# Letting the last batch's slots enter the slot product as one-hot products, in a kernel of clustered attention and a routed mixture of experts

## Chip, cores and metric

The kernel runs on one core of a Trainium2 chip. The metric is the device time of one execution in microseconds (us), as the median of several runs. About 0.2% of it, 1.5 us, can be told from no change.

## What is computed

The reference, cut to what matters here. `B, H, S, D = 4, 8, 768, 64`, so there are N = 3072 tokens of 512 values; 16 clusters; 4 groups of 4 experts, each with `w1` of 512 x 1024 and `w2` of 1024 x 512.

```python
# attention, for every batch and head
mask = q_assign[:, :, :, None] == k_assign[:, :, None, :]      # nearest centroids
scores = np.where(mask, scale * q @ k.T, -1e9)
x = softmax(scores) @ v                                        # -> tokens (N, 512)
# experts
for g in range(4):
    for e in range(4):
        ye = np.maximum(x[mine] @ w1[g, e], 0.0) @ w2[g, e]    # tokens whose group is g and expert e
        out[mine] = (g_w * e_w)[mine, None] * ye
```

## The kernel before

**Attention** (`attention`) goes through 32 heads of 9 units each; a unit is a piece of scores, its exponential (`exp` on ScalarE) and the product with V, and what is done beside the units (`beside`) is handed out unit by unit: a generator that yields once goes on one unit later. When the four head pairs of a batch are done, its 768 tokens are stored to `xbuf` in DRAM and routed.

**Routing** (`Router.decide`): for each batch the expert of each token is found, and its place among all tokens of its expert. The table in DRAM has for each expert a list of slots, and a slot holds a token's number and its gate. Each batch writes its entries by six scatters from GpSimd's queue (line 685, 128 tokens each, `table<-pay,rdi`). Empty slots hold the number N and the gate 0.

**Experts** (`Experts`). After three of the four batches, `first` picks the expert with most tokens so far. Beside the last batch's attention it loads and splits that expert's weights into high and low halves (`split_beside`), reads its list of 288 slots back (`tabA`), casts it to `idA` and `gA` (lines 849 and 850), gathers the tokens and turns them into `xTA`. When attention ends, **part A** (`part_a`) runs this expert on these slots: eight steps of `up` (line 963) and eight of `down` (line 985). Beside part A, the last batch is routed, `order` ranks the other experts by their number of tokens, and the stream of their weights starts (`stream`, line 767, six chunks of 512 KB ahead, which waits for `ei`, the ranked list). **Part B** then runs the first expert on its tokens of the last batch, which are picked by one-hot products (`slots_b`, `tokens_b`, lines 1107 to 1133) and never leave the chip. After it, `ranks` goes through the other experts, rank 0 to 14, with 288 slots down to 160; overflow is left to a loop at the end.

The lists of all ranks come from one place, the **slot product** (`slots`, line 1143): `tb`, the first 384 slots of each expert read back from the table (line 1113), times the permutation `perm` of the ranks, into one bank of PSUM. `columns` casts the result to `ri` and `rg` (lines 1053 and 1054), and the three gathers of rank 0 (line 925) start. `tb` is read behind all 24 scatters (`R.reads`).

The order on each engine is fixed when the program is built, by a scheduler that works with estimated times; `issue_after(ins)` adds that what is issued inside it on the engine of `ins` comes behind `ins`. `with self.after():` does this with the last `exp`. The wait lists, queues and buffers do the rest at run time: an engine's queue and SP's queue of transfers are in order, and `st` has four buffers, later six.

Of the kernel before, what the change touches and what calls it, by code (L numbers as in the profile page):

```python
# [22 lines left out]
P = 128  # L23
# [8 lines left out]
LAND = 4  # L32
# [496 lines left out]
class Router:  # L529
# [98 lines left out]
    def decide(self, b, early=None, then=None):  # L628
        nc, sm, E = self.nc, self.sm, self.E
        T = self.N // self.B // P  # L630
        t0 = b * T
        G = T * 5
        lv, eq, oh, df = (self.lg[b][:, n * G * 4:(n + 1) * G * 4].rearrange("p (g x) -> p g x", x=4) for n in range(4))
        mx = sm.tile([P, G], F32, name="rmx")
        nc.vector.tensor_reduce(out=mx, in_=lv, axis=AX.X, op=ALU.max)
        nc.vector.tensor_tensor(out=eq, in0=lv, in1=mx.broadcast_to([P, G, 4]), op=ALU.is_ge)
        nc.vector.tensor_tensor(out=eq, in0=eq, in1=self.desc[:, 0:G], op=ALU.mult)
        mw = sm.tile([P, G], F32, name="rmw")
        nc.vector.tensor_reduce(out=mw, in_=eq, axis=AX.X, op=ALU.max)
        nc.vector.tensor_tensor(out=oh, in0=eq, in1=mw.broadcast_to([P, G, 4]), op=ALU.is_equal)  # L640
        oh = oh.rearrange("p (t g) x -> p t g x", g=5)
        oe = sm.tile([P, T, 4, 4], F16, name="roe")
        og = sm.tile([P, T, 4], F32, name="rog")
        nc.vector.tensor_copy(out=og, in_=oh[:, :, 0])
        nc.vector.tensor_tensor(out=oe, in0=oh[:, :, 1:5], in1=og.broadcast_to([P, T, 4, 4]), op=ALU.mult)
        nc.vector.tensor_tensor(out=df, in0=lv, in1=mx.broadcast_to([P, G, 4]), op=ALU.subtract)
        nc.scalar.activation(out=df, in_=df, func=AF.Exp, scale=1.0 / (XS * WRS))
        se = sm.tile([P, T, 5], F32, name="rse")
        nc.vector.tensor_reduce(out=se.rearrange("p t g -> p (t g)"), in_=df, axis=AX.X, op=ALU.add)
        ss = sm.tile([P, T, 4], F32, name="rss")  # L650
        nc.vector.tensor_tensor(out=ss, in0=se[:, :, 1:5], in1=oh[:, :, 0], op=ALU.mult)
        yield
        es = sm.tile([P, T], F32, name="res")
        nc.vector.tensor_reduce(out=es, in_=ss, axis=AX.X, op=ALU.add)
        nc.vector.tensor_scalar(out=es, in0=es, scalar1=1e-9, scalar2=None, op0=ALU.add)
        nc.vector.scalar_tensor_tensor(out=es, in0=se[:, :, 0], scalar=1e-9, in1=es, op0=ALU.add, op1=ALU.mult)
        nc.vector.reciprocal(out=self.pay[:, t0:t0 + T, 1], in_=es)
        yield PSM, 1, 1
        o16 = oe.rearrange("p t g x -> p (t g x)")
        rk = self.psm.tile([P, 512], F32, name="psm")  # L660
        W = T * E
        nc.tensor.matmul(out=rk[:, 0:W], lhsT=self.low, rhs=o16, start=True, stop=False, skip_group_check=True)
        for s in range(1, T):
            nc.tensor.matmul(out=rk[:, s * E:W], lhsT=self.ones, rhs=o16[:, 0:W - s * E], start=False, stop=False, skip_group_check=True)
        for c in range(T):
            nc.tensor.matmul(out=rk[:, W:W + E], lhsT=self.ones, rhs=o16[:, c * E:(c + 1) * E], start=False, stop=c == T - 1, skip_group_check=True)
        yield
        ps = sm.tile([P, T, E], F32, name="rps")
        nc.vector.tensor_tensor(out=ps, in0=rk[:, 0:W].rearrange("p (t e) -> p t e", e=E), in1=self.cb.unsqueeze(1).broadcast_to([P, T, E]), op=ALU.add)
        nc.vector.tensor_tensor(out=ps, in0=ps, in1=oe.rearrange("p t g x -> p t (g x)"), op=ALU.mult)  # L670
        ds_ = self.rows = sm.tile([P, T], F32, name="rds")
        nc.vector.tensor_reduce(out=ds_, in_=ps, axis=AX.X, op=ALU.add)
        di = sm.tile([P, T], I32, name="rdi", bufs=2)
        self.last["v"] = nc.vector.tensor_copy(out=di, in_=ds_)
        nc.vector.tensor_tensor(out=self.cb, in0=rk[:, W:W + E], in1=self.cb, op=ALU.add)
        if early:
            early()
        if then:
            then()
        for c in range(T):  # L680
            for _ in range(1 if early else 4 if then else 5):
                yield

            with self.tc.issue_after(self.cfg["lo"].ins) if self.apart and not early and "lo" in self.cfg else ExitStack():
                d = self.last["p"] = nc.gpsimd.indirect_dma_start(
                    out=self.table, out_offset=bass.IndirectOffsetOnAxis(ap=di[:, c:c + 1], axis=0),
                    in_=self.pay[:, t0 + c], in_offset=None)
            if self.apart:

                self.alone(d, "sent", self.sent)  # L690
        self.done = b
# [17 lines left out]
class Experts:  # L709
# [4 lines left out]

    CA, CB = 288, 128
    AHEAD = 6
    SLOTS = 13
    SLT = 12
    FILL, SETTLE, TOK = (0, 1, 2, 3, 4, 5, 6, 7), 2, 5
# [20 lines left out]
    def setup(self):  # L740
        nc, const, E = self.nc, self.const, self.R.E
        self.io = const.tile([P, E], F32, name="io")
        nc.gpsimd.iota(self.io, [[1, E]], base=0, channel_multiplier=0, allow_small_or_imprecise_dtypes=True)
        self.capr = const.tile([1, E], F32, name="capr")
        i = 0
        while i < E:
            j = i
            while j < E and self.caps[j] == self.caps[i]:
                j += 1
            nc.gpsimd.memset(self.capr[:, i:j], float(self.caps[i]))  # L750
            i = j


    def part(self, i, q):
# [50 lines left out]
    def first(self):  # L805
# [15 lines left out]
        yield  # L821
        self.f0 = self.load_reg(self.f0i[0:1, 0:1], E - 1)
        self.WA = self.wtiles(self.wa, 0)
        chunks = []
        for q in range(4 + LAND):
            if q < 4:
                chunks.append(self.load_chunk(0, self.f0, q))
            if q >= LAND:
                yield from self.split_beside(chunks[q - LAND], *self.WA, 0, q - LAND)
            for _ in range(FIRST):  # L830
                yield

        CA, KD = self.CA, R.KD
        nt = -(-CA // P)
        sz = [min(P, CA - t * P) for t in range(nt)]
        tab = self.small("tabA", [P, nt, 2])
        tv = R.table.rearrange("(e s) w -> e s w", s=R.BS)[bass.ds(self.f0, 1)].rearrange("e s w -> (e s) w")
        w2A = [self.load_chunk(1, self.f0, q) for q in range(4)]
        self.WA += self.wtiles(self.wa, 1)
        while R.done < R.B - 2:  # L840
            yield
        for t, n in enumerate(sz):
            R.reads(nc.sync.dma_start(out=tab[0:n, t], in_=tv[t * P:t * P + n]))
        for _ in range(FIRST + 8):
            yield
        ids = self.small("idA", [P, nt], I32)
        g = self.small("gA", [P, nt])
        for t, n in enumerate(sz):
            nc.vector.tensor_copy(out=ids[0:n, t:t + 1], in_=tab[0:n, t, 0:1])
            nc.vector.tensor_scalar(out=g[0:n, t:t + 1], in0=tab[0:n, t, 1:2], scalar1=1.0 / (XS * WS * WS), scalar2=None, op0=ALU.mult)  # L850
        self.colsA = [g[0:n, t:t + 1] for t, n in enumerate(sz)], [ids[0:n, t:t + 1] for t, n in enumerate(sz)]

        rows = R.N - R.N // R.B
# [1 line left out]
        for t, n in enumerate(sz):  # L855
# [3 lines left out]
            if rows:  # L859
                with self.tc.issue_after(self.cfg["lo"].ins) if "lo" in self.cfg else ExitStack():  # L860
                    self.gather(ids[0:n, t:t + 1], n, xgs[t], rows)
            yield from self.split_beside(w2A[t], *self.WA[2:4], 1, t)
        for q in range(nt, 4):
            yield from self.split_beside(w2A[q], *self.WA[2:4], 1, q)
        xTA = self.wa.tile([P, KD, 2, CA], F16, name="xTA")
# [194 lines left out]
    def order(self):  # L1060
# [9 lines left out]
        nc.vector.scalar_tensor_tensor(out=key, in0=self.oh0, scalar=-1e7, in1=key, op0=ALU.mult, op1=ALU.add)  # L1070
        gt = sm("gt", [P, E, E], F16)
        nc.vector.tensor_tensor(out=gt, in0=key.unsqueeze(1).broadcast_to([P, E, E]), in1=key.broadcast_to([P, E, E]), op=ALU.is_gt)
        rank = sm("rank", [P, E])
        nc.vector.tensor_reduce(out=rank, in_=gt, axis=AX.X, op=ALU.add)
        pr = self.pr = sm("pr", [1, E, E])
        iob = self.io[0:1].broadcast_to([1, E, E])
# [17 lines left out]
    def slots_b(self):  # L1094
# [13 lines left out]
        nc.scalar.copy(out=self.o16, in_=o32)  # L1108
        self.o32, self.pb = o32, pb
        next(self.fill)  # L1110
        nt = self.nt = -(-max(self.caps) // P)
        self.tb = self.stage2.tile([P, 2, 512], F32, name="tb", bufs=1).rearrange("p a b -> p (a b)")[0:E, 0:2 * nt * P].rearrange("e (s w) -> e s w", w=2)
        R.reads(nc.sync.dma_start(out=self.tb, in_=R.table.rearrange("(e s) w -> e s w", s=R.BS)[0:E, 0:nt * P]))

    def tokens_b(self):

# [19 lines left out]
    def slots(self):  # L1136
# [3 lines left out]
        tpv = tps[:, 0:2 * nt * E].rearrange("p (w t e) -> p w t e", w=2, t=nt)  # L1140
        for t_ in range(nt):
            for w in range(2):
                nc.tensor.matmul(out=tpv[:, w, t_], lhsT=tb[:, t_ * P:(t_ + 1) * P, w], rhs=perm, start=True, stop=True)
        self.ids, self.gates = self.columns([tpv[:, 0], tpv[:, 1]], [P, nt, E], "r")
        self.xg0 = self.gathers(0)

# [229 lines left out]
def tile_cluster_attention_moe(ctx, tc, qT, kT, vr, cen, wr, w1, w2, out):  # L1376
# [33 lines left out]
    for _ in R.decide(B - 1, early=X.order):  # L1410
        pass
    X.slots_b()
    for i, _ in enumerate(ga):
        with tc.issue_after(X.mm.ins):
            if i == X.SLOTS:
                X.slots()
            if i == X.SLT:
                X.xTB = X.tokens_b()
# [38 lines left out]
```

## Time and profile before

| | |
|---|---|
| median of 3 runs | 769.58 us (769.55 to 770.92) |
| profiled execution, its own time | 770.8 us |
| its span, first to last instruction | 768.7 us |
| PE busy, matmuls (PE) and weight loads (PEld) | 94% and 81% |
| VectorE (DVE), ScalarE (ACT), GpSimd (POOL) busy | 78%, 58%, 64% |
| mean granted clock of PE | 0.981 |
| moved by DMA | 134.75 MB, 175 GB/s on average |

The trace counts from the first instruction of the span. Attention fills it to some 417 us, part A to some 457, part B to some 467 and the ranks the rest. A busy share is a mean over these stages, which have different limits, so the rows below are of single stretches.

### The profile page before, as it was taken

What the parts mean: (1) busy time and instruction counts of PE and PEld (TensorE: products, weight loads), DVE (VectorE), ACT (ScalarE), POOL (GpSimd) and SP (SyncE); (2) the same over time, 40 slices, a digit from 0 to 9 for tenths busy, and PEclk for the clock granted to TensorE, in tenths of its full rate; (3) what the DMA queues carried; (4) which work ended last, traced back from release to release, by engine and by line L of the source; (5) the groups of instructions that cost most, each with busy time, mean ns of one, the idle gap of its engine ahead of it and who ended that gap; (6) DMA issues with size and microseconds to landing.
All of it is one profiled execution on the core that took longest, in us unless ns stands there. A gap on an engine that the chain in (4) does not pass through costs nothing. (4 is left out here: it accounts for less than half of the span.)

```text
span 768.7 us, 26315 instructions
## 1 busy us (share of the span) xinstructions
PE 724.7 (94%) x10882; PEld 619.0 (81%) x10882; DVE 598.9 (78%) x1194; ACT 444.6 (58%) x877; POOL 495.7 (64%) x522
## 2 busy tenths in 40 slices
PE   5898999999999999997898979999999999999996
PEld 3676888888888888876776857888779999999896
DVE  5997988899798988996665545868588988888761
ACT  4567867677686777755674246444534455555542
POOL 9568687889978998787852435426555555554433
PEclk9999999999999999999989979999999999999998
DMA  8759647467653765407422487866677788788721
GB/s 248 190 157 217 161 125 158 111 145 185 125 162 91 173 146 104 97 12 178 127 63 61 55 269 275 275 210 216 226 245 239 255 255 274 256 279 276 248 75 49
DMA packets 115719, 134.75 MB, mean 175 GB/s; under 512 B 34963, under 2 KB 85651, under 8 KB 115592
## 3 DMA queue, kind: packets, MB, share of 16 engines
q1 hardware_dynamic: 109820, 119.61, 56.7%
q0 software_dynamic: 5616, 13.35, 4.9%
q8 instruction: 87, 1.43, 0.8%
q14 instruction: 40, 0.33, 0.2%
q10 hardware_dynamic: 156, 0.03, 0.0%
HBM read 93.20 MB, written 14.11 MB: 140 GB/s over the span
## 5 line engine op out<-in xcount | busy, mean ns | idle before, releaser
L354 POOL TENSOR_TENSOR pl<-p 128x512 f16<-128x512 f32 x278 | 285.6, 1047 | 80.8 <-ACT p L352 75.8
L308 DVE TENSOR_REDUCE mpart<-psc 128x1 f32<-128x512 f32 (+1 forms) x282 | 190.0, 683 | 29.2 <-PE psc L305 28.5
L352 ACT ACTIVATE p<-psf 128x512 f32<-128x512 f32 x288 | 168.5, 593 | 76.5 <-PE psf L348 69.4
L373 PE MATMUL pso<-V,p 128*128 128x65 f16 x1152 | 164.0, 195 | 0.0
L373 PE MATMUL pso<-V,pl 128*128 128x65 f16 x1152 | 163.2, 195 | 0.0
L374 PE MATMUL pso<-V,p 128*128 128x64 f16 x1152 | 162.9, 192 | 0.0
L374 PE MATMUL pso<-V,pl 128*128 128x64 f16 x1152 | 162.6, 192 | 0.0
L347 PE MATMUL psf<-A 82*128 82x384 f16 (+2 forms) x576 | 145.9, 278 | 6.4 <-ACT p L352 3.8
L348 PE MATMUL psf<-B 128*128 128x384 f16 (+2 forms) x576 | 146.1, 278 | 0.0
L374 PEld LDWEIGHTS <-p 128*128 128x128 bf16 x1152 | 113.6, 99 | 21.1 <-issue 1.0
L373 PEld LDWEIGHTS <-p 128*128 128x128 bf16 x1152 | 113.2, 98 | 12.6 <-issue 4.6
L305 PE MATMUL psc<-A 80*128 80x512 f16 (+1 forms) x376 | 109.9, 334 | 5.3 <-DVE mpart L308 4.2
L374 PEld LDWEIGHTS <-pl 128*128 128x128 f16 x1152 | 113.7, 99 | 0.6 <-issue 0.2
L373 PEld LDWEIGHTS <-pl 128*128 128x128 f16 x1152 | 112.1, 97 | 0.3
L966 DVE SCALAR_TENSOR_TENSOR hl<-psh,hh 128x160 f16<-128x160 f32 (+14 forms) x136 | 50.2, 371 | 60.5 <-ACT hh L965 60.1
L965 ACT ACTIVATE hh<-psh 128x160 f16<-128x160 f32 (+14 forms) x136 | 46.5, 347 | 62.5 <-PE psh L963 62.2
L963 PE MATMUL psh<-xT,wh0a 128*128 128x288 f16 (+7 forms) x512 | 74.7, 255 | 0.0
L348 PEld LDWEIGHTS <-B 128*128 128x128 f16 x576 | 57.4, 100 | 15.8 <-issue 6.6
L925 POOL DMA_INDIRECT xg<-xbuf,ri x32 | 42.2, 1318 | 40.9 <-issue 19.8
L963 PE MATMUL psh<-xT,wh0b 128*128 128x272 f16 (+6 forms) x448 | 65.2, 254 | 1.3 <-DVE xT L937 0.7
L347 PEld LDWEIGHTS <-A 82*128 82x128 f16 x576 | 56.2, 99 | 11.5 <-DMA A<-mr 2.2
L963 PE MATMUL psh<-xT,wl0a 128*128 128x288 f16 (+7 forms) x256 | 64.0, 255 | 0.0
(303 smaller groups left out, 1688.4 us busy)
## 6 DMA issues: line engine op xcount, KB each, us to landing
st<-w SPq DMA_DIRECT2D x128, 512.0 KB
B<-parts SPq DMA_DIRECT2D x64, 192.0 KB
kx<-kT SPq DMA_DIRECT2D x16, 384.0 KB
qx<-qT SPq DMA_DIRECT2D x16, 384.0 KB
vx<-vr SPq DMA_DIRECT2D x16, 384.0 KB
A<-parts SPq DMA_DIRECT2D x32, 192.0 KB
xbuf<-xs SPq DMA_DIRECT2D x16, 384.0 KB
A<-mk SPq DMA_DIRECT2D x56, 24.0 KB
```

Of the source, the lines that this page charges most:

```text
L305: last["mm"] = nc.tensor.matmul(out=pc[:, off:off + k1 - k0], lhsT=QA[h % 8][0:80, c * P:(c + 1) * P], rhs=KA[h % 8][0:80, k0:k1], start=T ...
L308: nc.vector.tensor_reduce(out=(mp[:, 0, 0:1], mp[:, :, 1], mp[:, 1, 0:1])[i], in_=pc.rearrange("p (a x) -> p a x", a=n), axis=AX.X, op=ALU ...
L347: nc.tensor.matmul(out=o, lhsT=KA[h % 8][0:82, ks], rhs=QA[h % 8][0:82, q0:q1], start=True, stop=False)
L348: nc.tensor.matmul(out=o, lhsT=KBs[h][:, ks], rhs=QBs[h][:, q0:q1], start=False, stop=True)
L352: cfg["exp"] = nc.scalar.activation(out=p32, in_=pf, func=AF.Exp, scale=QK / (SQ * SQ))
L354: lo = (nc.vector if u in (EARLY if h < 2 else DVE_LO[h % 8] if h < NH - 2 else DVE_END) else nc.gpsimd).tensor_tensor(out=pl, in0=p32, in ...
L373: nc.tensor.matmul(out=O[:, col:col + 65], lhsT=p[:, bs], rhs=vh, start=c == 0 and q == 0 and i == 0, stop=False, skip_group_check=True)
L374: nc.tensor.matmul(out=O[:, col:col + 64], lhsT=p[:, bs], rhs=vl, start=False, stop=c == NCH - 1 and i == 1, skip_group_check=True)
L925: self.got = nc.gpsimd.indirect_dma_start(out=xg[0:n].rearrange("p k a x -> p (k a x)"), out_offset=None, in_offset=bass.IndirectOffsetOnA ...
L963: self.mm = nc.tensor.matmul(out=ph[:, 0:M], lhsT=w[:, k, fs], rhs=xT[:, a, k], start=i == 0, stop=i == 3 * KD - 1)
L965: nc.scalar.activation(out=hh[:, f], in_=ph[:, 0:M], func=AF.Relu)
L966: self.ev = nc.vector.scalar_tensor_tensor(out=hl[:, f], in0=ph[:, 0:M], scalar=0.0, in1=hh[:, f], op0=ALU.max, op1=ALU.subtract)
```

## The change

The table is read into `tb` beside attention, when three batches are in it, and the fourth batch's entries are added to the slot product on TensorE:

- `slots_new` makes, on VectorE, for each of the last batch's six chunks of 128 tokens a one-hot of the slot within its expert (`oS`, 128 x 288) and a one-hot of its expert's rank times the token's number minus N and its gate. The number is cut into two and the gate into three bfloat16 parts (`sw`, three pairs). The pieces are handed out from step 5 of part A on.
- `slots` adds 54 matmuls (6 chunks x 3 slot tiles x 3 pairs) onto the product of `tb` and `perm`, in the same bank.
- The read of `tb` moves from `slots_b` into `first`, behind the gathers of part A's tokens, and its buffer out of the pool `stage2`.
- In `first`, the loads of the second weight matrix stand one by one behind the splits of the first one, no longer in one row behind all of them. The read of `tabA` comes one unit later, the casts after four units instead of ten and under `self.after()`.
- The last batch's six scatters stay, for the overflow loop.

```diff
@@ class Experts
+    ADD = 5
@@ setup
+        T = self.R.N // self.R.B // P
+        self.io16 = const.tile([P, max(self.caps)], F16, name="io16")
+        nc.gpsimd.iota(self.io16, [[1, max(self.caps)]], base=0, ...)
+        self.svals = const.tile([P, T, 3, 2], BF16, name="svals")
+        nc.gpsimd.memset(self.svals, 0.0)
+        nc.gpsimd.iota(self.svals[:, :, 0, 0], [[P, T]], base=-P * T, ...)
+        nc.gpsimd.iota(self.svals[:, :, 1, 0], [[0, T]], base=0, channel_multiplier=1, ...)
@@ first
             for _ in range(FIRST):
                 yield
+            if q >= LAND:
+                w2A.append(self.load_chunk(1, self.f0, q - LAND))
...
-        w2A = [self.load_chunk(1, self.f0, q) for q in range(4)]
         self.WA += self.wtiles(self.wa, 1)
         while R.done < R.B - 2:
             yield
+        yield
         for t, n in enumerate(sz):
             R.reads(nc.sync.dma_start(out=tab[0:n, t], in_=tv[t * P:t * P + n]))
-        for _ in range(FIRST + 8):
+        for _ in range(LAND):
             yield
...
-        for t, n in enumerate(sz):
-            nc.vector.tensor_copy(out=ids[0:n, t:t + 1], in_=tab[0:n, t, 0:1])
-            nc.vector.tensor_scalar(out=g[0:n, t:t + 1], in0=tab[0:n, t, 1:2], ...)
+        with self.after():
+            for t, n in enumerate(sz):
+                nc.vector.tensor_copy(out=ids[0:n, t:t + 1], in_=tab[0:n, t, 0:1])
+                nc.vector.tensor_scalar(out=g[0:n, t:t + 1], in0=tab[0:n, t, 1:2], ...)
...
+        self.nt = -(-max(self.caps) // P)
+        self.tb = self.small("tb", [R.E, self.nt * P, 2])
+        R.reads(nc.sync.dma_start(out=self.tb, in_=R.table...[0:R.E, 0:self.nt * P]))
@@ slots_b
-        nt = self.nt = -(-max(self.caps) // P)
-        self.tb = self.stage2.tile([P, 2, 512], F32, name="tb", bufs=1)...
-        R.reads(nc.sync.dma_start(out=self.tb, in_=R.table...[0:E, 0:nt * P]))
+    def slots_new(self):
+        nc, R, E, vals = self.nc, self.R, self.R.E, self.svals
+        T = R.rows.shape[1]
+        g = R.pay[:, R.N // P - T:, 1]
+        oe = R.oe.rearrange("p t g x -> p t (g x)")
+        x = self.small("sx", [P, T, E])
+        s = self.small("sslot", [P, T])
+        nc.vector.tensor_tensor(out=x, in0=oe, in1=R.ebase...., op=ALU.mult)
+        nc.vector.tensor_reduce(out=s, in_=x, axis=AX.X, op=ALU.add)
+        nc.vector.tensor_tensor(out=s, in0=R.rows, in1=s, op=ALU.subtract)
+        yield
+        self.oS = self.xp.tile([P, T, max(self.caps)], F16, name="hh")
+        for c in range(T):
+            nc.vector.tensor_scalar(out=self.oS[:, c], in0=self.io16, scalar1=s[:, c:c + 1], scalar2=None, op0=ALU.is_equal)
+            if c % 3 == 2:
+                yield
+        r = self.small("sg", [P, T])
+        nc.vector.tensor_copy(out=vals[:, :, 0, 1], in_=g)
+        nc.vector.tensor_tensor(out=r, in0=g, in1=vals[:, :, 0, 1], op=ALU.subtract)
+        nc.vector.tensor_copy(out=vals[:, :, 1, 1], in_=r)
+        nc.vector.tensor_tensor(out=r, in0=r, in1=vals[:, :, 1, 1], op=ALU.subtract)
+        nc.vector.tensor_copy(out=vals[:, :, 2, 1], in_=r)
+        yield
+        nc.vector.tensor_tensor(out=x, in0=oe, in1=self.rank...., op=ALU.mult)
+        rho = self.small("srank", [P, T])
+        nc.vector.tensor_reduce(out=rho, in_=x, axis=AX.X, op=ALU.add)
+        nc.vector.tensor_tensor(out=x, in0=self.io...., in1=rho...., op=ALU.is_equal)
+        yield
+        self.sw = self.small("sw", [P, T, 6, E], BF16)
+        nc.vector.tensor_tensor(out=self.sw, in0=x...., in1=vals...., op=ALU.mult)
@@ slots
-                nc.tensor.matmul(out=tpv[:, w, t_], lhsT=tb[:, t_ * P:(t_ + 1) * P, w], rhs=perm, start=True, stop=True)
+                nc.tensor.matmul(out=tpv[:, w, t_], lhsT=tb[...], rhs=perm, start=t_ + w == 0, stop=False, ...)
+        for t_ in range(nt):
+            for c in range(T):
+                for i in range(3):
+                    lhsT = self.oS[:, c, t_ * P:min((t_ + 1) * P, self.oS.shape[2])]
+                    nc.tensor.matmul(out=tpv[0:lhsT.shape[1], :, t_], lhsT=lhsT, rhs=self.sw[:, c, 2 * i:2 * i + 2], start=False, stop=c == T - 1 and i == 2, ...)
@@ main program
     X.slots_b()
+    new = X.slots_new()
     for i, _ in enumerate(ga):
         with tc.issue_after(X.mm.ins):
+            if i >= X.ADD:
+                next(new, None)
             if i == X.SLOTS:
```

## Rows read from the trace of the kernel before

**Rows 1.** The page's first line.
```profile
span 768.7 us, 26315 instructions
```

**Rows 2.** Windows over seven stretches; the header names the columns, PEclk is the granted clock.
```profile
core 0: us, PE busy (x) PEld busy (x) DVE busy (x) ACT busy (x) POOL busy (x), PEclk, DMA share, GB/s
385.00:391.90 6.90, 6.52 (x83) 5.19 (x83) 3.87 (x8) 2.64 (x6) 3.08 (x3) 0.51 0.01 2
408.90:412.30 3.40, 3.40 (x28) 2.46 (x27) 1.25 (x2) 2.43 (x5) 2.08 (x2) 0.50 0.00 0
434.00:440.00 6.00, 6.00 (x69) 5.14 (x67) 0.92 (x2) 0.82 (x2) 3.57 (x5) 1.00 0.99 152
443.90:449.10 5.20, 0.00 (x0) 0.00 (x0) 1.88 (x4) 2.79 (x4) 0.00 (x0) 0.75 0.87 226
449.10:456.70 7.60, 7.55 (x33) 5.76 (x34) 2.95 (x5) 0.00 (x0) 3.10 (x3) 0.50 0.78 247
486.00:680.00 194.00, 193.94 (x1998) 174.78 (x1996) 157.25 (x237) 91.88 (x183) 99.57 (x88) 1.00 0.77 248
680.00:724.00 44.00, 42.09 (x569) 41.24 (x567) 36.32 (x56) 21.30 (x49) 24.43 (x23) 1.00 0.80 266
```

**Rows 3.** Timeline of PE: start us, us, instruction, count, idle before and its releaser.
```profile
360.02 0.61 PE L609 MATMUL psm<-WR,xTr 128*128 128x20 f16 x18 [2.61 <-DMA xTr<-xs]
...
383.64 0.38 PE L305 MATMUL psc<-A 80*128 80x512 f16 x1 [2.45 <-DVE mpart L308]
...
407.50 0.41 PE L963 MATMUL psh<-xTA,wh 128*128 128x288 f16 x2 [2.38 <-DMA xTA<-vx]
...
412.97 0.60 PE L609 MATMUL psm<-WR,xTr 128*128 128x20 f16 x18
...
449.15 2.71 PE L1143 MATMUL psm<-perm,tb 16*128 16x16 f32 x12 [5.27 <-DMA tb<-table]
...
457.13 0.28 PE L963 MATMUL psh<-xT,wh 128*128 128x128 f16 x2
...
462.21 1.35 PE L935 MATMUL psm<-ident,xg 128*128 128x128 f16 x24
...
466.93 0.29 PE L963 MATMUL psh<-xT,wh0a 128*128 128x288 f16 x1
```

**Rows 4.** The chain of waits, 434 to 449 us: start us, us, what.
```profile
434.80 11.10 DMA table<-pay,rdi
...
446.01 3.01 DMA tb<-table
```

**Rows 5.** Timeline of VectorE (DVE), columns as in rows 3.
```profile
382.77 0.15 DVE L849 CAST idA<-tabA 128x1 int32<-128x1 f32 x1 [4.10 <-DMA tabA<-table]
...
428.50 0.27 DVE L1107 TENSOR_SCALAR st<-sl,rds 128x128 f32<-128x128 f32 x1
...
444.97 0.68 DVE L1126 CAST xT<-psm 128x512 f16<-128x512 f32 x1
...
451.90 0.21 DVE L1053 CAST ri<-psm 128x48 int32<-128x48 f32 x1 [6.12 <-PE psm L1143]
...
452.50 2.35 DVE L777 SCALAR_TENSOR_TENSOR wl0a<-st,wh0a 128x1024 f16<-128x1024 f32 x2
```

**Rows 6.** Line 609, 405 to 460 us: durations in ns, minimum, median, maximum.
```profile
L609 PEld LDWEIGHTS <-xTr x36: 95/96/99, 412.9 to 421.6; 128*128 128x128 f16 x36
L609 PE MATMUL psm<-WR,xTr x36: 171/171/185, 413.0 to 421.7; 128*128 128x20 f16 x36
```

**Rows 7.** Timeline of POOL, columns as in rows 3.
```profile
393.97 1.34 POOL L925 DMA_INDIRECT qx<-xbuf,idA  x1 [0.15 <-issue]
...
456.15 0.88 POOL L925 DMA_INDIRECT xg<-xbuf,ri  x1 [0.30 <-issue]
```

**Rows 8.** Line 925, the gathers of 440 to 480 us.
```profile
DMA to landing us min/median/max: 4.9/5.9/6.7
```

**Rows 9.** Timeline of SP's queue, columns as in rows 3.
```profile
356.14 8.51 SPq L767 DMA_DIRECT2D st<-w  x2
```

More of the change, by code (lines that the diff above doesn't have):

```diff
@@ L641, in decide @@
         oh = oh.rearrange("p (t g) x -> p t g x", g=5)
-        oe = sm.tile([P, T, 4, 4], F16, name="roe")
+        oe = self.oe = sm.tile([P, T, 4, 4], F16, name="roe")
         og = sm.tile([P, T, 4], F32, name="rog")
@@ L751, in setup @@
             i = j
+        T = self.R.N // self.R.B // P
+        self.io16 = const.tile([P, max(self.caps)], F16, name="io16")
+        nc.gpsimd.iota(self.io16, [[1, max(self.caps)]], base=0, channel_multiplier=0, allow_small_or_imprecise_dtypes=True)
+        self.svals = const.tile([P, T, 3, 2], BF16, name="svals")
+        nc.gpsimd.memset(self.svals, 0.0)
+        nc.gpsimd.iota(self.svals[:, :, 0, 0], [[P, T]], base=-P * T, channel_multiplier=0, allow_small_or_imprecise_dtypes=True)
+        nc.gpsimd.iota(self.svals[:, :, 1, 0], [[0, T]], base=0, channel_multiplier=1, allow_small_or_imprecise_dtypes=True)
     def part(self, i, q):
@@ L823, in first @@
         self.WA = self.wtiles(self.wa, 0)
-        chunks = []
+        chunks, w2A = [], []
         for q in range(4 + LAND):
@@ L847, in first @@
         g = self.small("gA", [P, nt])
-        for t, n in enumerate(sz):
-            nc.vector.tensor_copy(out=ids[0:n, t:t + 1], in_=tab[0:n, t, 0:1])
-            nc.vector.tensor_scalar(out=g[0:n, t:t + 1], in0=tab[0:n, t, 1:2], scalar1=1.0 / (XS * WS * WS), scalar2=None, op0=ALU.mult)
+        with self.after():
+            for t, n in enumerate(sz):
+                nc.vector.tensor_copy(out=ids[0:n, t:t + 1], in_=tab[0:n, t, 0:1])
+                nc.vector.tensor_scalar(out=g[0:n, t:t + 1], in0=tab[0:n, t, 1:2], scalar1=1.0 / (XS * WS * WS), scalar2=None, op0=ALU.mult)
         self.colsA = [g[0:n, t:t + 1] for t, n in enumerate(sz)], [ids[0:n, t:t + 1] for t, n in enumerate(sz)]
@@ L862, in first @@
             yield from self.split_beside(w2A[t], *self.WA[2:4], 1, t)
+        self.nt = -(-max(self.caps) // P)
+        self.tb = self.small("tb", [R.E, self.nt * P, 2])
+        R.reads(nc.sync.dma_start(out=self.tb, in_=R.table.rearrange("(e s) w -> e s w", s=R.BS)[0:R.E, 0:self.nt * P]))
         for q in range(nt, 4):
@@ L1072, in order @@
         nc.vector.tensor_tensor(out=gt, in0=key.unsqueeze(1).broadcast_to([P, E, E]), in1=key.broadcast_to([P, E, E]), op=ALU.is_gt)
-        rank = sm("rank", [P, E])
+        rank = self.rank = sm("rank", [P, E])
         nc.vector.tensor_reduce(out=rank, in_=gt, axis=AX.X, op=ALU.add)
@@ L1110, in slots_b @@
         next(self.fill)
-        nt = self.nt = -(-max(self.caps) // P)
-        self.tb = self.stage2.tile([P, 2, 512], F32, name="tb", bufs=1).rearrange("p a b -> p (a b)")[0:E, 0:2 * nt * P].rearrange("e (s w) -> e s w", w=2)
-        R.reads(nc.sync.dma_start(out=self.tb, in_=R.table.rearrange("(e s) w -> e s w", s=R.BS)[0:E, 0:nt * P]))
+    def slots_new(self):
[5 more added lines that the diff above has]
+        s = self.small("sslot", [P, T])
+        nc.vector.tensor_tensor(out=x, in0=oe, in1=R.ebase.unsqueeze(1).broadcast_to([P, T, E]), op=ALU.mult)
+        nc.vector.tensor_reduce(out=s, in_=x, axis=AX.X, op=ALU.add)
[13 more added lines that the diff above has]
+        yield
+        nc.vector.tensor_tensor(out=x, in0=oe, in1=self.rank.unsqueeze(1).broadcast_to([P, T, E]), op=ALU.mult)
+        rho = self.small("srank", [P, T])
+        nc.vector.tensor_reduce(out=rho, in_=x, axis=AX.X, op=ALU.add)
+        nc.vector.tensor_tensor(out=x, in0=self.io.unsqueeze(1).broadcast_to([P, T, E]), in1=rho.broadcast_to([P, T, E]), op=ALU.is_equal)
+        yield
+        self.sw = self.small("sw", [P, T, 6, E], BF16)
+        nc.vector.tensor_tensor(out=self.sw, in0=x.unsqueeze(2).broadcast_to([P, T, 6, E]), in1=vals.rearrange("p t i w -> p t (i w)").broadcast_to([P, T, 6, E]), op=ALU.mult)
     def tokens_b(self):
@@ L1142, in slots @@
             for w in range(2):
-                nc.tensor.matmul(out=tpv[:, w, t_], lhsT=tb[:, t_ * P:(t_ + 1) * P, w], rhs=perm, start=True, stop=True)
+                nc.tensor.matmul(out=tpv[:, w, t_], lhsT=tb[:, t_ * P:(t_ + 1) * P, w], rhs=perm, start=t_ + w == 0, stop=False, skip_group_check=True)
+        T = R.rows.shape[1]
+        for t_ in range(nt):
+            for c in range(T):
+                for i in range(3):
+                    lhsT = self.oS[:, c, t_ * P:min((t_ + 1) * P, self.oS.shape[2])]
+                    nc.tensor.matmul(out=tpv[0:lhsT.shape[1], :, t_], lhsT=lhsT, rhs=self.sw[:, c, 2 * i:2 * i + 2], start=False, stop=c == T - 1 and i == 2, skip_group_check=True)
         self.ids, self.gates = self.columns([tpv[:, 0], tpv[:, 1]], [P, nt, E], "r")
```

## Prediction

> **What bounds the kernel now.** Of the 768.7 us of the profiled execution [rows 1] PE is busy nearly all, and the page alone would say "PE bound, nothing to gain". So I read the windows first. They show that PE runs without a pause and at the full clock from 486 to 680 us [rows 2], so whatever makes PE start that stretch earlier moves everything behind it. [...] The timeline of PE names the place: line 1143, the slot product, starts at 449.15 after 5.27 us of idle, so PE had come there at 443.88 [rows 3]. The chain of waits names the reason: the transfer `table<-pay,rdi`, 11.10 us from its issue at 434.80, and behind it `tb<-table`, 3.01 us [rows 4]. So the six scatters of the last batch and the reading back of the table are what PE waits for in the middle of part A.
>
> Two smaller holes lie in the attention part. PE stands 2.45 us at 383.64, waiting for a VectorE reduction, and 2.38 us at 407.50, waiting for the transposed tokens `xTA` [rows 3]. After each the clock is at 0.50 to 0.51 for 6.9 and 3.4 us [rows 2]. The first has its cause on VectorE: the cast `idA` stood 4.10 us at the head of its queue until `tabA` landed, with the reductions behind it [rows 5].
>
> **The removed wait.** After the change, the table is read while only 18 scatters are behind it, long before 443.88. What does PE wait for then? Lines 1125 and 1129 and the slot product take their banks in turn from a pool of three, after `rk` of decide. Counting on from `rk`, the slot product takes the bank of the first product of line 1125, and VectorE empties that one at 444.97 + 0.68 = 445.65 [rows 5]. The 5.27 us shrink to 445.65 - 443.88 = 1.77 us, not to nothing.
>
> **The added matmuls.** Six chunks by three slot tiles by three parts are 54, with 128 x 128 weights and 32 columns. The nearest row is line 609: 18 matmuls with 20 columns in 0.60 us, of which the last one's 0.17 us is latency, so 0.43 / 17 = 25 ns each [rows 3, 6]. With 32 columns I take 28 ns: 1.5 us. The bound above is that no weight load overlaps anything: 54 x 96 ns = 5.2 us [rows 6]. I stay at 1.5, since line 609 issues a load of 96 ns for every matmul and still goes at 25 ns.
>
> [...]
>
> **PE up to the end of part A.** The twelve passes of line 1143 took 2.71 us at half clock [rows 3]; at full clock 1.36. From 449.15 + 2.64 = 451.79 to 457.13 the last 24 matmuls of line 985 took 5.34 us, of which all but the last 0.4 lay at half clock: 2.9 at full clock. An idle of 1.77 us is below the 2.38 to 5.2 us behind which the clock fell here, so I count full clock. New end: 445.65 + 1.36 + 1.5 + 2.9 = 451.4, against 457.13: 5.7 us earlier.
>
> **What is late next: the gathers of rank 0.** Its slot list leaves the slot product, VectorE casts it (line 1053, 451.90), and POOL issues three gathers, the third at 456.15, 4.25 us after the cast began [rows 5, 7]. The cast now begins at 445.65 + 1.36 + 1.5 + 0.05 = 448.6, the third gather at 452.8, and it lands 5.9 us later (4.9 to 6.7) [rows 8]: 458.7. PE needs it for the last eight transposes of line 935, which start 5.08 us after the end of part A [rows 3], some 0.4 of it in waits, plus 0.9 us for the two tiles before: 451.4 + 4.6 + 0.9 = 456.9 to 457.4. A new wait of about 1.3 us (0.3 to 2.1) appears. Left: 5.7 - 1.3 = 4.4 us.
>
> **Does it last to the end?** The first weights of rank 0 are split by 452.50 + 2.35 = 454.85 [rows 5], and before the change PE comes to them at 466.93 [rows 3], 12 us later, so they are ready. The weight stream itself moves too: its sixth load stood on SP's queue behind `tb`, issued at 446.01 [rows 4]; now only its buffer holds it, which is `o32`, read last by line 1129, ahead of PE's hole at 443.88. From 486 to 680 PE is full and DMA is at 0.77 [rows 2], so there is room; from 680 to 724 PE has 1.9 us of gaps, where the stream is just in time. I count 4.4 us as kept; if the stream did not follow, it would go there.
>
> **VectorE's new work.** Eighteen operations. Twelve at the 0.27 us of a 128-wide row and six over 288 columns at most 0.27 x 288 / 128 = 0.6: 3.2 + 3.6, at most some 7 us [rows 5]. Between 434 and 440 VectorE is busy for 0.92 of 6 us [rows 2], and PE needs the results at 445. Cost nothing; if they were put ahead of `ei`, which starts the weight stream, the stream would be late by some of it, inside the 12 us above. The four POOL operations in setup, by the same rule at most 0.6 each and 2.4 together, once and near the start, and the issue of `tb` on SP I count at nothing, since POOL and SP are not what PE waits for in any of the holes; bound 2.4 us.
>
> **The list of part A.** Two edits. The casts now stand under `after()`, which ties instructions to the last `exp`. `exp` is issued by `nc.scalar` and the casts run on VectorE [rows 5], and issue_after orders within one engine, so I expect no tie and the wait of 4.10 us to stay: 0. If it did bind, it would give up to 2.45 + 6.9 / 2 = 5.9 us. Second, ten units of waiting become four (and one before the read), so gathers and weight splits start some five units earlier than 393.97 [rows 7], and `xTA` is ready up to 8 us before PE stands at 407.50. This can remove 2.38 + 3.4 / 2 = 4.1 us. But the matmuls that wait there have a fixed place in PE's queue, which is made anew with the program and may lie as much earlier, with the same wait: 0. The trace can't tell; I take half, 2.0.
>
> **Sum.** 4.4 + 2.0 = 6.4 us. The profiled execution took 770.8 us (span 768.7 [rows 1] and some 2 around it), so its like would take 764.4; the median is 769.58, 1.2 below, which gives 763.2. A measurement of this kernel can tell about 0.2%, 1.5 us.
>
> **Rivals.**
> (a) Another wait takes the place: VectorE puts the third weight split ahead of emptying the bank, with a load to wait for, or the weight stream does not follow and PE gives the time back from 680 to 724; the attention part stays. For it speaks that VectorE empties the bank only at 444.97, late for matmuls that ended before 443.88; against it, that PE has no gap from 486 to 680 and so waits for no weights there [rows 2]. 767 to 769.6.
> (b) All holes go: the tie does work (5.9) and `xTA` is early (4.1), with the slots' 4.4: 14 us, 755; with one of them wholly, 758. Against it: the engines of `exp` and cast.
> (c) Weight loads in the row: 3.7 us more on PE, and the list and its gathers late by as much: 763.2 + 3.7 = 766.9. Against it: line 609.
> (d) Slower: the loads of the second weight matrix now stand between the first one's splits on SP's queue, and each waits there for a buffer. One pair took SP 8.51 us already at 356.14 [rows 9]; a transfer that comes late costs as much as at 360.02, where PE waited 2.61 us for `xTr` [rows 3]; with 3.4 us at the lower clock behind it, as behind 407.50 [rows 2], 2.6 + 1.7 = 4.3 us a time. One such stall eats the 4.4; from the second on the kernel is slower, 769.6 - 4.4 + 2 x 4.3 = 773.8 without gain at `xTA`, 771 to 775. For it: SP is in order. Against it: the buffers are free at the same moments as before.
>
> **How the numbers follow.** Forecast (slots' gain, none to all of the 4.1): 0.55, 758.5 to 767. (a) 0.17, (b) 0.10, (c) 0.05, (d) 0.13. Below 768.0 lie the forecast, (b), (c) and 0.10 of (a): faster 0.80; 0.07 of (a) and 0.01 of (d) are no change, 0.08; slower 0.12. The range 757 to 770 leaves out (d) and most of (b), 0.2.
>
> **What would show it.** Right: `tb` is read before 410 us; ahead of the slot product PE waits 1 to 2 us, for VectorE's copy and not for a DMA; 54 matmuls in some 1.5 us; the clock stays at 1.00 from 444 to 457; a wait of 1 us at line 935; part A's end near 451 less whatever attention gained; `idA` still waits some 4 us; at `xTA` no wait or a shorter one. Wrong: `idA` no longer waits (b), the 54 take 5 us (c), PE waits for `xTr` or `A` between 350 and 400 (d), or the gain is there at 486 and gone at 724 (a).

## The result, and the profile after

The changed kernel takes 760.07 us (median of 4 runs, 759.25 to 761.65), the kernel before in the same runs 770.12: a ratio of 0.9873, 95% interval 0.9839 to 0.9908. The profiled execution has a span of 757.8 us, 10.9 below that of before.

PE's timeline after the change, columns as in [rows 3]:

```profile
384.12 0.59 PE L305 MATMUL psc<-A 80*128 80x512 f16 x1 [3.26 <-DVE mpart L308]
...
439.90 1.58 PE L1186 MATMUL psm<-perm,tb 16*128 16x16 f32 x12 [1.33 <-DVE xT L1169]
441.42 1.70 PE L1192 MATMUL psm<-sw,hh 128*128 128x32 bf16 x54
443.05 2.10 PE L999 MATMUL psy<-hh,wh 128*128 128x288 f16 x8
...
447.06 0.27 PE L977 MATMUL psh<-xT,wh 128*128 128x128 f16 x2
...
452.13 1.35 PE L949 MATMUL psm<-ident,xg 128*128 128x128 f16 x24
...
456.85 0.41 PE L977 MATMUL psh<-xT,wh0a 128*128 128x288 f16 x2
```

The wait for `tb` ahead of the slot product, 5.27 us in [rows 3], is now 1.33 us and is ended by VectorE's copy. The wait for `xTA` at the start of part A has no row any more. The wait at 384 is still there and longer. Part A ends at 447.06, 10.07 us earlier than the 457.13 of [rows 3], and rank 0 starts 10.08 earlier: line 949 waits for nothing.

Windows over the stretches that answer to [rows 2], with its columns:

```profile
383.81:387.22 3.41, 3.10 (x34) 2.43 (x34) 3.18 (x12) 2.23 (x4) 1.04 (x1) 0.50 0.06 15
438.60:439.90 1.30, 0.00 (x0) 0.00 (x0) 1.30 (x5) 0.75 (x2) 0.00 (x0) 1.00 0.95 269
441.83:445.25 3.42, 3.42 (x55) 2.54 (x51) 1.50 (x4) 1.06 (x1) 1.01 (x1) 0.50 1.06 371
480.00:680.00 200.00, 199.94 (x2097) 181.53 (x2095) 163.36 (x245) 96.15 (x194) 107.36 (x95) 1.00 0.78 250
```

The granted clock is at 0.50 for 3.4 us behind 384, where it was at 0.51 for 6.9 [rows 2], and at 0.50 for 3.4 us from 441.8, which was not expected. From 480 to 680 PE is full (199.94 of 200.00 us, at 1.00), as before, so what was won ahead of it is kept.

VectorE, then SP's queue and GpSimd, of the same execution:

```profile
383.25 0.15 DVE L860 CAST idA<-tabA 128x1 int32<-128x1 f32 x1 [4.91 <-DMA tabA<-table]
...
438.02 1.23 DVE L785 SCALAR_TENSOR_TENSOR wl0a<-st,wh0a 128x1024 f16<-128x1024 f32 x1 [0.18 <-ACT wh0a L782]
439.16 0.68 DVE L1169 CAST xT<-psm 128x512 f16<-128x512 f32 x1
```

```profile
383.57 0.43 SPq L876 DMA_DIRECT2D tb<-table  x1
...
387.24 1.07 POOL L939 DMA_INDIRECT qx<-xbuf,idA  x1 [0.15 <-issue]
```

The cast of `idA` still stands 4.91 us at the head of VectorE's queue (4.10 in [rows 5]). `tb` is read at 383.57, and the first gather of part A's tokens leaves at 387.24 where it left at 393.97 [rows 7]. Ahead of the slot product VectorE does a weight split and then the copy that empties the bank, 439.16 + 0.68 = 439.84.

The 54 added matmuls, with their weight loads (ns: minimum, median, maximum):

```profile
L1192 PEld LDWEIGHTS <-hh x54: 95/103/114, 441.4 to 442.9; 128*128 128x128 f16 x36, 128*32 128x32 f16 x18
L1192 PE MATMUL psm<-sw,hh x54: 176/188/209, 441.4 to 442.9; 128*128 128x32 bf16 x36, 128*32 128x32 bf16 x18
```

Eighteen of them, those of the last slot tile, have weights of 32 columns and not of 128.

### The profile page after: what moved, and what is told of

The parts are those of the page before. It is cut to its first block, busy times and chain, and to the rows that moved or that the text cites. A ratio compares the mean times of both kernels' runs of the same rounds, so it can differ in the third digit from the quotient of the medians.

```text
span 757.8 us, 26445 instructions
## 1 busy us (share of the span) xinstructions
PE 719.5 (95%) x10936; PEld 616.1 (81%) x10936; DVE 604.5 (80%) x1212; ACT 444.7 (59%) x877; POOL 495.7 (65%) x526
## 4 chain that ended last, share of the span: by engine, by line
PE 60%; DVE 11%; DMA 10%; ACT 7%; issue 4%; POOL 4%; SPq 2%; POOLq 0%; ACTq 0%; DVEq 0%
PE psh L977 15%; PE psy L999 11%; PE pso L373 5%; PE psf L347 5%; PE psf L348 5%; PE pso L374 5%; PE psc L305 5%; PE psy L1013 3%; POOL pl L354 3%; DMA st<-w 3%; DVE mpart L308 3%; ACT p L352 2%; DMA B<-parts 2%; DMA xTr<-xs 2%; PE psm L1039 1%
## 5 line engine op out<-in xcount | busy, mean ns | idle before, releaser
L308 DVE TENSOR_REDUCE mpart<-psc 128x1 f32<-128x512 f32 (+1 forms) x282 | 190.0, 683 | 27.7 <-PE psc L305 26.9
L347 PE MATMUL psf<-A 82*128 82x384 f16 (+2 forms) x576 | 144.2, 276 | 6.1 <-ACT p L352 4.6
L348 PE MATMUL psf<-B 128*128 128x384 f16 (+2 forms) x576 | 144.5, 276 | 0.0
```

What stands on the lines that cost most here:

```text
L308: nc.vector.tensor_reduce(out=(mp[:, 0, 0:1], mp[:, :, 1], mp[:, 1, 0:1])[i], in_=pc.rearrange("p (a x) -> p a x", a=n), axis=AX.X, op=ALU ...
L347: nc.tensor.matmul(out=o, lhsT=KA[h % 8][0:82, ks], rhs=QA[h % 8][0:82, q0:q1], start=True, stop=False)
L348: nc.tensor.matmul(out=o, lhsT=KBs[h][:, ks], rhs=QBs[h][:, q0:q1], start=False, stop=True)
```

## The experiments

Each time is the median beside the kernel before on the same chip; ratios have 95% intervals. The runs fell on three chips, here called the second to the fourth; the chip of the first pair of traces is called the first (whether it is one of the three is not recorded). The intervals reach 0.2 to 0.4% to either side, so a difference has to be of up to 3 us to be told from none, not of the 1.5 us named at the start. A trace is of one execution, and not always of a typical one: that of before on the third chip took 760.93 us against a median of 765.94, slots alone on the second 777.14 against 770.70, and the tied casts on the fourth 765.19 against 761.34. The first pair, 770.8 and 759.5, lies near its medians.

| kernel | second chip | third chip | fourth chip |
|---|---|---|---|
| before, us | 770.51 | 765.94 | 772.03 |
| changed | | 759.19; 0.9914 (0.9884 to 0.9944) | 769.20; 0.9946 (0.9915 to 0.9977) |
| slots alone | 770.70; 1.0006 (0.9979 to 1.0034) | | 772.37; 1.0002 (0.9980 to 1.0024) |
| lists alone | 766.55; 0.9955 (0.9923 to 0.9986) | | 765.52; 0.9910 (0.9874 to 0.9947) |
| changed, casts tied | 761.41; 0.9901 (0.9866 to 0.9937) | | 761.34; 0.9844 (0.9810 to 0.9878) |
| changed, other bank | 767.29; 0.9955 (0.9934 to 0.9976) | 757.23; 0.9906 (0.9873 to 0.9939) | |
| changed, both | | 754.98; 0.9848 (0.9810 to 0.9885) | |

**What needed no run.** The changed program and the same one without `self.after()` hold the same instructions in the same order with the same waits on every engine: the tie does nothing. A program of before with only the loads of the second weight matrix moved is also the same, engine by engine, as the kernel before. So of the list edits only the units count: the four units instead of ten, and the one ahead of the read.

**The two parts alone.** Slots alone, against the changed kernel:

```diff
@@ first
-            if q >= LAND:
-                w2A.append(self.load_chunk(1, self.f0, q - LAND))
...
+        w2A = [self.load_chunk(1, self.f0, q) for q in range(4)]
...
-        yield
         for t, n in enumerate(sz):
             R.reads(nc.sync.dma_start(out=tab[0:n, t], ...))
-        for _ in range(LAND):
+        for _ in range(FIRST + 8):
             yield
...
-        with self.after():
```

> The changed kernel with the list of part A put back as it was (the second weight matrix's loads in a row, no unit more before the read, ten units after it, no tie): the slot part alone. Theory, the two parts are separate and add up: attention runs as in the kernel before (part A's first eviction within 0.3 us of it), the wait of 5.27 us ahead of the slot product shrinks to 1 to 2 us, part A ends 4.0 to 4.8 us earlier, and the total is 4.4 to 5.3 us below the kernel before: about 765. Rival 1, the slot part carries most of the gain and the list edits only share it: 8 us or more below. Rival 2, the weight stream needs the attention part's 5.7 us to be in time, so that without the list edits PE gives the slots' gain back between 680 and 724 us: within 1 us of the kernel before.

Lists alone is the kernel before with the change's edits to the list of part A; the read of `tb` stays in `slots_b`, and there is no `slots_new` and none of the 54 matmuls.

> The kernel before with the edits to the list of part A alone (loads of the second weight matrix one by one, one unit more before the read of the list, four units instead of ten behind it, the tie); the table is read back after the last scatters as before, and no one-hot products are made. Theory, the lists alone give what was seen in the attention part: no wait for the transposed tokens of part A, 3.4 us of lower clock instead of 6.8 behind the wait at 384, part A's first eviction 5.5 to 6.0 us earlier, and the wait ahead of the slot product still 5 us because the scatters move along with part A; total 5 to 6 us below, about 764.5. Rival 1, the prediction's term: 2.0 us below. Rival 2, the slots' wait grows by what attention gained because the table's way is fixed in time: 0.

On the second chip slots alone gave nothing (0.9979 to 1.0034) and lists alone 0.45%. The first has the time of its second rival, but not by that rival's cause, since nothing is given back from 680 to 724 (from rank 0's first eviction to the end it takes 298.6 us, before 299.3). The second, 4.0 us, falls between the theory (5 to 6) and the first rival (2.0). But these traces hold a stall that neither of the first two has, so all was run again beside controls.

> The kernel before itself, for a trace on the same chip as the three below: four traces of variants showed a stall of 4 to 5 us of PE, with ScalarE's eviction told late, between 424 and 440 us, and two more of 1 to 2 us behind part A, which neither the trace before nor the one after has. If these belong to the chip of that hour and not to the variants, this trace has them too (770 to 775 us); if they belong to the variants, it looks like the trace before (769 to 771).

> The changed kernel itself, as a control. If the stalls belong to the chip: it has them here, and its time is 3 to 6 us above the 760.1 us first measured, about the 767.3 of the variant with the other bank. If they belong to the variants: 759.3 to 761.7 and a trace like the first.

The third chip has no such stall, in either of the two controls, and the change gives 0.86% there, 6.8 us; the kernel before takes 765.94 us, less than the 769 to 771 expected. PE's timeline of before on it, then of the changed kernel:

```profile
383.14 0.38 PE L305 MATMUL psc<-A 80*128 80x512 f16 x1 [3.18 <-DVE mpart L308]
...
405.15 0.41 PE L963 MATMUL psh<-xTA,wh 128*128 128x288 f16 x2 [2.54 <-DMA xTA<-vx]
...
443.10 1.55 PE L1143 MATMUL psm<-perm,tb 16*128 16x16 f32 x12 [2.91 <-DMA tb<-table]
```

```profile
438.40 1.58 PE L1186 MATMUL psm<-perm,tb 16*128 16x16 f32 x12 [0.21 <-DVE xT L1169]
439.91 1.61 PE L1192 MATMUL psm<-sw,hh 128*128 128x32 bf16 x54
441.45 1.15 PE L999 MATMUL psy<-hh,wh 128*128 128x288 f16 x8
...
451.10 0.51 PE L949 MATMUL psm<-ident,xg 128*128 128x128 f16 x6 [0.64 <-DMA xg<-xbuf,ri]
```

The same waits are there in other sizes: 2.91 us for the table instead of 5.27, 0.21 for the bank instead of 1.33. And where the bank is hardly a hold-up, the gathers of rank 0 are one, by 0.64 us, as the prediction had it (1.3, 0.3 to 2.1).

> The changed kernel itself, as the control for the three below, on the same chip. From the two chips on which it was measured so far: 6 to 10 us below the kernel before.

> The slot part alone, again, beside the changed kernel. Theory: on a chip where the signals between the engines come in time, PE goes through part A's second half without a stall, and the slot part is worth what the wait and the lower clock behind it were worth, 4 to 5 us below the kernel before. Rival, what was seen in the first trace of it is the rule, and the slot part only trades the wait for the table for another: within 1.5 us of the kernel before.

> The list edits alone, again. Theory: the wait for the transposed tokens (2.4 to 2.7 us) always goes, and with it the lower clock behind it in those executions that have it: 2.5 to 4.1 us below the kernel before, and together with the slot part alone the whole of the change to within 1.5 us. Rival 1, the two share one gain: each alone is worth nearly the whole. Rival 2, the lists alone are worth 5.7 us, as the first pair of traces has it.

On the fourth chip slots alone gives nothing again, lists alone 0.90%, and the change 0.54%, which is 2.8 us and not the 6 to 10 that were expected. The parts do not add up: 6.5 us of the lists, more than the 2.5 to 4.1 expected, and nothing of the slots stand against 2.8. Two traces show a part of the reason. PE's timeline of the changed kernel there:

```profile
426.24 0.29 PE L977 MATMUL psh<-xTA,wl 128*128 128x288 f16 x1
426.36 0.65 PE L999 MATMUL psy<-hh,wh 128*128 128x288 f16 x4
431.12 0.28 PE L999 MATMUL psy<-hh,wh 128*128 128x288 f16 x1 [4.10 <-ACT hh L979]
```

ScalarE's timeline of the same execution, and the windows, which on the third chip have 4.00 of 4.00 us of PE between 427 and 431:

```profile
430.65 0.41 ACT L979 ACTIVATE hh<-psh 128x288 f16<-128x288 f32 x1 [5.46 <-remote]
```

```profile
427.00:431.00 4.00, 0.01 (x1) 0.00 (x0) 0.19 (x1) 0.35 (x1) 3.54 (x5) 1.00 0.71 30
431.68:435.10 3.42, 3.42 (x16) 2.15 (x15) 2.03 (x10) 0.16 (x1) 0.00 (x0) 0.50 0.74 211
```

The eviction of the last piece of `up` waits for a group of matmuls that ended at 426.24 + 0.29 = 426.53, but starts at 430.65: the signal between the two is 4.1 us late ("remote" says that no instruction shown ended the wait). VectorE and PE stand too, and the clock falls behind it (0.50 from 431.68 to 435.10). In lists alone on the same chip the late signal comes one piece of work later, at the first eviction of `down`, where PE has a second bank to go on in, and the table is waited for as in the kernel before; PE's timeline, and the row of ScalarE:

```profile
432.83 0.65 PE L988 MATMUL psy<-hh,wh 128*128 128x288 f16 x4 [0.91 <-DVE yl L992]
...
442.01 1.55 PE L1146 MATMUL psm<-perm,tb 16*128 16x16 f32 x12 [2.09 <-DMA tb<-table]
```

```profile
431.87 0.71 ACT L991 ACTIVATE yh<-psy 128x288 f16<-128x288 f32 x2 [4.95 <-remote]
```

So with the slot part PE loses 4.10 us and 3.42 / 2 = 1.7 for the clock, and does 1.6 us of new matmuls: 7.4. (Half of a stretch at 0.50 is an estimate: in the first trace of the changed kernel eight matmuls of line 999 took 2.10 us at 0.50, at 443.05, and 1.14 us at 1.00, at 446.08.) Without it, it loses 0.91 + 2.09, and 1.7 for 3.4 us of lower clock from 444.2: 4.7. The slot part costs 2.7 us in these two traces, and from the last exponential to part B's first eviction they differ by 43.37 - 40.72 = 2.65. The medians, 769.20 and 765.52, lie the same way, with intervals that overlap. In these traces the wait that the slot part removes is one in which another wait lay hidden. That the kernel before has the same two waits is argued from lists alone, since no trace of it was taken on the second and fourth chip; and slots alone against it shows no loss there (0.9980 to 1.0024, at most 1.9 us), so the 2.7 us are not shown for the old list.

Cutting all traces at two marks (the starts of the 265th and the last row of line 352, the exponential, and of part B's first eviction) shows both parts at once, in us:

| traces | 265th to last exponential | last exponential to part B |
|---|---|---|
| old list (4) | 31.8, 33.9, 36.3, 36.9 | |
| new list (7) | 30.1, 30.6, 30.7, 30.9, 31.3, 32.1, 32.4 | |
| new list, casts tied (3) | 26.4, 26.8, 27.7 | |
| old slots, first and third chip (2) | | 44.5, 40.2 |
| new slots, first and third chip (4) | | 40.2, 37.9, 39.3, 39.3 |
| old slots, second and fourth (2) | | 41.5, 40.7 |
| new slots, second and fourth (6) | | 42.1, 43.1, 43.2, 43.4, 43.4, 43.8 |

The new list is worth 34.7 - 31.2 = 3.5 us on average, though the lowest of the old (31.8) lies below the highest of the new (32.4). The 6.5 us of lists alone on the fourth chip are more than that; the rest is not explained. No trace with the new list waits for `xTA`, all four with the old one do, for 2.38 to 2.67 us; the rest is how long the clock stays low behind 384 (3.4 or 6.8 us with either list, 0 in one trace of the old one) and behind that wait (3.4 us in two of the four). Neither part was run alone on a chip without the late signals: what each is worth there, 4.3 and 2.3 us for the slots in the two pairs of traces, rests on these cuts.

**The casts really tied.** Against the changed kernel:

```diff
@@ coarse
-        nc.vector.tensor_reduce(out=(mp[:, 0, 0:1], ...)[i], ...)
+        cfg["red"] = nc.vector.tensor_reduce(out=(mp[:, 0, 0:1], ...)[i], ...)
@@ first
-        for _ in range(LAND):
+        for _ in range(6):
             yield
...
-        with self.after():
+        with self.tc.issue_after(self.cfg["red"].ins):
```

> The changed kernel, but the casts of the list of part A are tied to VectorE's own latest reduction of the scores (not to the exponential, which runs on ScalarE) and come six units after the read instead of four, so that five reductions stand ahead of them. Theory, the casts at the head of VectorE's queue are what keeps PE waiting at 384: the casts wait less than 0.5 us, PE's gap of 3.26 us there goes and the 3.4 us of lower clock behind it too, 3.26 + 1.7 = 5.0 us below the changed kernel: about 755. Rival 1, the gap goes but the clock falls there all the same: 3.3 us below, 757. Rival 2, PE then waits for something else in these 5 us (a row of maxima, the transposed tokens, the exponential), or the later list makes the transposed tokens late at part A: within 1 us of the changed kernel, 759 to 761.

> The changed kernel with the casts tied to VectorE's own reduction, again, beside the changed kernel. Theory from the first trace of it: 5 us or more below the changed kernel. Rival, from the trace with both edits: the wait of 3 us at 384 goes, but a wait of 1.4 us for a row of maxima takes its place, and 2 to 3 us are left.

VectorE's timeline on the fourth chip, and the row of PE that now holds the wait there:

```profile
383.78 0.69 DVE L308 TENSOR_REDUCE mpart<-psc 128x1 f32<-128x512 f32 x1 [0.39 <-PE psc L305]
384.39 0.14 DVE L860 CAST idA<-tabA 128x1 int32<-128x1 f32 x1
```

```profile
384.80 0.34 PE L347 MATMUL psf<-A 82*128 82x384 f16 x1 [0.57 <-DMA A<-mr]
```

The cast waits for nothing, PE's gap is gone and with it the lower clock behind it; in its place is a wait of 0.57 us for a row of maxima (1.38 in the kernel with both edits). From the 265th exponential to the last that is 31.2 - 27.0 = 4.2 us, and on the fourth chip 769.20 - 761.34 = 7.9 us between the medians, with intervals that do not touch (0.9810 to 0.9878 against 0.9915 to 0.9977). That the casts at the head of the queue made PE wait is shown: the gap is gone in all three traces with this edit. How much beyond 4.2 us is theirs is not, and the second chip's 761.41 us (about 755 was expected) stands without a changed kernel beside it; nor were the tie and the two more units tried apart.

**Another bank for the slot product.** Against the changed kernel:

```diff
@@ slots
-        tps = self.R.psm.tile([P, 512], F32, name="psm")
+        tps = next(self.ps_h).tile([P, 512], F32, name="psh")
```

> The changed kernel, but the slot product takes its bank from the three of the up products, which stand free there, instead of the bank that VectorE empties last for the tokens of part B. Theory, the 1.33 us of idle time ahead of the slot product is that bank alone, and the 3.4 us at the lower clock from 441.8 follow from that idle time: both go, 1.33 + 1.7 = 3.0 us below the changed kernel, about 757. Rival 1, the idle time goes but the lists and gathers of rank 0 are then late by about as much at line 949, as the prediction had it: 1.3 to 1.7 us below. [...] Rival 3, PE then waits for the one-hot products or for the table instead of the bank: no change.

> The changed kernel with the slot product in a bank of the up products, again, now beside the changed kernel on one chip. Theory: 3.0 us below the changed kernel on the same chip (1.33 us of idle time and 1.7 us of lower clock). Rival 1: 1.3 us below, since the clock falls for other reasons. Rival 2, the other bank itself brought the stalls: 6 us above.

PE's timeline on the third chip, then two windows of it:

```profile
437.94 1.58 PE L1186 MATMUL psh<-perm,tb 16*128 16x16 f32 x12
439.45 1.61 PE L1192 MATMUL psh<-sw,hh 128*128 128x32 bf16 x54
440.99 1.75 PE L999 MATMUL psy<-hh,wh 128*128 128x288 f16 x8
```

```profile
437.94:441.40 3.46, 3.46 (x71) 3.29 (x71) 2.53 (x8) 2.41 (x3) 0.00 (x0) 1.00 0.92 290
441.40:444.82 3.42, 3.42 (x17) 2.19 (x15) 1.15 (x2) 0.00 (x0) 2.19 (x2) 0.50 0.98 320
```

No idle time is left, and the clock falls all the same. The theory, that the fall follows from the idle time, is wrong. Of the ten traces with the 54 matmuls three have a fall there (the first of the changed kernel with 1.33 us idle ahead, and the third chip's two with the other bank with none), and seven have none, six of them without idle time ahead. What decides it is open. The times say no more: 757.23 against 759.19 with intervals that overlap by most of their width, so that neither 3.0 nor 1.3 us is told from nothing. The run on the second chip had no changed kernel beside it.

**Both edits**, on the third chip.

> The changed kernel with both: the casts tied to VectorE's own reduction six units after the read, and the slot product in a bank of the up products. Theory, the two are separate: 5.0 + 3.0 = 8 us below the changed kernel on the same chip, about 752 where it takes 760. Rival 1, with the attention part earlier the weights of rank 0 are the next thing late, and the second gain is lost: 5 us below. Rival 2, the tie gives nothing: 3 us below.

754.98 us, 4.2 below the changed kernel and 11.0 below the kernel before (0.9848, 0.9810 to 0.9885): with the tied casts alone on the fourth chip (0.9844) the largest gain of this study, though not the 8 us over the changed kernel that were expected. The tied casts were not run alone on the third chip, so the share of the bank in the 4.2 us is not known. PE's row at 386 has a wait for maxima where the casts' wait was:

```profile
385.95 0.34 PE L347 MATMUL psf<-A 82*128 82x384 f16 x1 [1.38 <-DMA A<-mr]
```

## Why the prediction was right, point by point

The change took 10.05 us off in the first runs, 6.8 on the third chip and 2.8 on the fourth; the 6.4 that were forecast lie among them. That the first runs came out on the good side of the forecast, and that one of its terms came out to a tenth, is in part luck, as the points say.

- **The slots' 4.4 us.** In the first pair of traces the stretch behind attention is 44.46 - 40.16 = 4.3 us shorter, but not by the sum as it stood. The bank was the one forecast, emptied at 439.84 by the copy that was named, and held PE for 1.33 us instead of 1.77. The clock was counted as full and fell, so the last 24 matmuls of line 999 took 447.06 - 443.05 = 4.0 us, not 2.9. The wait for the gathers did not come, since PE itself was that much later; it came, 0.64 us, in the execution whose clock stayed up. So 1.1 us too little was counted for the clock and 1.3 too much for the gathers: that they cancel is luck. (The bounds of that wait, 0.3 to 2.1, go by 457.4 alone; by 456.9, which the prediction also gives, they reach 2.6.)
- **The 54 matmuls.** 1.5 forecast, 1.70 and 1.61 measured; without a latency of some 0.2 us (one of them takes 188 ns, the median above) that is 27 to 28 ns each, at weight loads of 95 to 114 ns in the first trace. The prediction had all of them at 128 x 128 weights; 18 are narrower, with loads no shorter (102 to 114 ns against 95 to 105). Rival (c) is out: with the loads in the row the 54 would take over 5 us (54 x 96 ns, an estimate from [rows 6]).
- **The list.** That the tie is none was right, and the cast's 4.91 us show it. The term for `xTA`, half of 4.1 us, was mis-sized: the wait went wholly, so that rival (b) came true for this half and not for the tie. In the first pair attention gives 5.8 us, of which 2.38 is this wait and 3.4 / 2 = 1.7 the clock behind it; the other 1.7 is the shorter stretch of lower clock behind 384, which traces with either list have in both lengths, so it is luck. The doubt behind "half" was the place of the matmuls that wait. It did move, but the other way: in the program before, two of them stand ahead of attention's last products (407.50 in [rows 3]; its last exponential starts at 414.13), so their wait held up attention too; in the changed one all stand behind attention's last product.
- **Rival (d)** had no ground: the order of SP's queue is the same with and without that edit.
- **Rival (a)** is what the second and fourth chip show for the slot part, another wait in place of the removed one, but one that was not on the list: an eviction told some 4 us late, most of which had lain within the wait for the table. The forecast rested on one execution of one chip and on the longest of the four waits for the table that were seen (5.27, 2.91, 2.80 and 2.09 us).
- **VectorE's new work at nothing.** VectorE is busy for 604.5 us instead of 598.9, and in none of the ten traces does PE wait for the one-hot products.
- **Kept to the end.** Part B begins 10.07 us earlier in the first pair and the span ends 10.9 earlier, so the weight stream followed. From rank 0's first eviction on, all fourteen traces take 297 to 300 us.

## What to carry to other kernels

A wait on the path may cover another that ends a little earlier: before a wait is priced, look for what else would end in it, and on more than one execution (on the fourth chip PE stood 0.91 us for the late eviction where it still waited 2.09 us for the table, and 4.10 us where it did not). A waiting instruction cost here what was queued behind it (the cast's 4.91 us became 3.26 of PE); the tie to ScalarE's exponential did nothing (the cast still waited 4.91 us), the one to VectorE's own reduction, with two more units, ended the wait: name an instruction of the same engine, and look at the order of the finished program to see whether a tie does anything. Test each half of a change alone: here one half carries the gain on the two chips where the halves ran alone, and the halves did not add up.

## What the runs showed of the hardware that was not expected

- Two of the chips had signals from PE to ScalarE that came late at one place, in all eight traces taken there (idle time of PE 2.7 to 4.15 us with the new slots, 0.8 to 0.9 with the old), and lost 3 to 7 us more between part B's first eviction and rank 0's (14.5 to 18.0 us there, 10.8 to 11.5 in all six traces on the other two). The changed kernel stalls on the fourth chip (4.10 us of PE) and not on the third (4.00 of 4.00 us busy from 427 to 431); each chip was used in one stretch of time, so chip and hour are not told apart. GpSimd and DMA go on meanwhile (3.54 of 4 us busy and a share of 0.71, above); what holds the signals is open.
- The clock fell to 0.50 right behind the slot product with no idle time ahead of it, in the third chip's traces with the other bank and with both edits, and stayed at 1.00 in that chip's control and in the six traces of the second and fourth chip, with the same work. Before the fall PE did 12 matmuls of 16 columns and 54 of 32, and was busy by the rows for all of it (3.46 of 3.46 us from 437.94 with the other bank).
